# Two sliding-window attention layers on one core: values paired with the next group's scores up to group 57, a planner's transfer model switched later, requests for product inputs moved

## The chip, the core and the metric

The kernel runs on one core of a Trainium2 chip. The metric is the device time of one execution in microseconds. Three runs before the change took 1801.02, 1803.50 and 1804.85 us; the median is 1803.5.

The core has five engines with instruction streams of their own: TensorE (PE for its matmuls, PEld for its weight loads), VectorE (DVE), ScalarE (ACT), GpSimd (POOL) and SyncE (SP). The last three also issue DMAs here. A stream is executed in order; semaphores tie the streams together.

## The reference

Two attention layers over 2048 rows of width 1024, with 32 heads of 32, all in float32. Both project the input, attend inside a window, and project again.

```python
def _A_ref(x, wqkv, wo):                 # H = 32, Dh = 32, W = 8, dil = 2
    qkv = (x @ wqkv).reshape(B, S, 3, H, Dh).transpose(2, 0, 3, 1, 4)
    q, k, v = qkv[0], qkv[1], qkv[2]
    idx = pos[:, None] - (jnp.arange(W) * dil)[None, :]        # 8 keys, every second row back
    kg, vg = k[:, :, idx_c, :], v[:, :, idx_c, :]
    logits = einsum("bhsd,bhswd->bhsw", q, kg) * Dh ** -0.5    # rows before 0 masked
    o = einsum("bhsw,bhswd->bhsd", softmax(logits), vg)
    return o.transpose(0, 2, 1, 3).reshape(B, S, D) @ wo

def _B_ref(x, wqkv, wo):                 # the same with a causal window of 256 rows
    scores = einsum("bhqd,bhkd->bhqk", q, k) * Dh ** -0.5
    mask = (i - j >= 0) & (i - j < 256)
    o = einsum("bhqk,bhkd->bhqd", softmax(where(mask, scores, -1e9)), v)
    return o.transpose(0, 2, 1, 3).reshape(B, S, D) @ wo

return jnp.concatenate([A, B], axis=-1)
```

## The kernel before

**Arithmetic.** A float32 operand of a projection is kept as two parts for TensorE, a high one (a rounding cast, line 276 on ACT or line 279 on DVE) and a low one (`raw` minus high, line 282, always DVE, 512 columns an instruction). Each projection step is three matmuls (`TERMS`: high x high, high x low, low x high). Here a **step** is such an item of the list `gemm`; where a place in the program is given as a number, it counts these steps from the start.

**Tiling.** Layer B runs first, then layer A. Each layer is cut into four units of 512 rows, so there are units 0 to 3 (B, dense window) and 4 to 7 (A; its rows are put in an order in which the dilated window is a band of eight neighbours). A unit has eight groups of four heads; group hg = 8u + s. Groups 32 to 63 belong to layer A. `DU` = 4 is the number of layer B's units.

**The list of projections.** `plan` sets the order of the steps: for each group a Q/K block `qk(u, s)` of two halves t = 0, 1 with eight steps each; `v` for values; for the unit pair 6 and 7 the values come from seven block products instead (`vp`, `value_product`, tiles `r` holding sums of inputs, adds at line 1007); `o` is the output projection of layer B; `p` are the output products of layer A (adds at line 902); `x` steps bring in a unit's inputs. Line 1101 and line 1133 build sums for these products. A last run of projections closes the kernel behind the values of group 63.

**The loads.** A `Stream` walks through the projections' operands in their order of use. `load_to` issues a 512 KB load into one of three buffers `raw` on POOL's queue (line 221); `split_to(n)` makes the two parts of all operands up to the n-th (`parts`), and when the low part is done the buffer is free and the load three further on is issued. Operands have kinds: `w` a weight tile, `x` an input tile, `xw` the sums for a product. `qk_items` holds the calls of `split_to` by which a Q/K block requests the operands behind it; `then` is the index of the first operand behind the block's own, and k the step of the half.

**A group in layer A** (`window`). Scores are 64 small matmuls into four banks (`s<-pbuf`). DVE and ACT then do a chain: four mask adds (line 1214), row maximum `nm` (1224), subtraction (1226), exp on ACT (1230), row sum `sm` (1238), reciprocal (1240), product (1242), a transpose (1244), and ACT's eight copies into `wide` (1253, 1256). Values (`o<-wide,vbuf`) are 20 matmuls, or 16 in a unit without rows ahead of it. Q and K reach the scores by a copy from PSUM to `nat` and a DMA on SP's queue into `pbuf` (`pbuf<-nat`, the seat). In layer B the keys go to `kst` by such DMAs.

**What sets the order.** The order of all engines is fixed when the program is built. A planner keeps a clock for each engine (class `Clock`, with a table of costs) and at each point takes the next step of the projections, the next scores or the next values, whichever is ready first. Its `ready` functions hold the rules. `PAIRED` appears in three of them: scores of a group below `PAIRED` wait until the group before has its weights in `wide`; values of a group are not issued before the scores of the next one, as long as that one is below `PAIRED`; and a scores item below `PAIRED` has its reserve of instructions raised by that of the values behind it.

```python
if hg + 1 < PAIRED and hg + 1 not in done["scores"]:
    return None
```

So up to group 49 the values of a group come directly behind the scores of the next; from 50 on each comes when it is ready.

**The transfers in the planner.** `marks` are two places in the list of steps. Between them `ck.traced` is set; then the planner takes a load's time from a model in which two queues share the transfer engines (`share`), outside from one in which transfers follow each other (`move`). The flag also picks the rule for POOL's use of the port that it has in common with DVE. It is a matter of what the planner expects; the program issues the same instructions either way.

Of the kernel before, what the change touches and what calls it, by code (L numbers as in the profile page):

```python
# [29 lines left out]
CHUNK, ASKED, LEFT, FETCHED = 256, 150, 290, 7.0  # L30
EXTRA, EACH = 246, 5.2
P_LATE = 1.5
PAIRED = 50
VPARTS = ((0,4),(4,2),(6,2))
V_SLOTS = {0:0,5:1,7:2}
O_SLOTS = {2: (0, 1), 3: (2, 3), 4: (4, 5), 5: (6, 7)}
# [255 lines left out]
def kernel(ctx, tc, xs, wqk, wv, wo, outs, units):  # L292
# [4 lines left out]
    DU = sum(u[2] for u in units)  # L297
# [21 lines left out]
    def mm(out, left, right, **k):  # L319
        issued[0] += 4 if left.dtype == F32 else 2  # L320
        n = int(issued[0] + EXTRA - ASKED) // CHUNK
        if n > asked[0]:
            asked[:] = n, ck.now
        nc.tensor.matmul(out, left, right, **k)  # L324
# [90 lines left out]
    for p in plan:  # L415
# [21 lines left out]
        else:  # L437
# [8 lines left out]
            else:  # L446
# [6 lines left out]
    st = Stream(nc, ck, raws, wpool, xpool, items, [more[:, 1024 * i:1024 * i + 1024] for i in range(3)],  # L453
                where[("qk",) + LIGHT_FROM + (0,)] if LIGHT_FROM[0] < U else len(items))
# [109 lines left out]
    def latest(*ts):  # L564
        return None if any(t is None for t in ts) else max(ts)


    def qk_items(u, s):
# [98 lines left out]
        for t in range(2):  # L667
            h = {}

            def ready(k, t=t, h=h):  # L670
                if k == 0:
                    st.split_to(where["qk", u, s, t] + 1)
                    w = st.ready[where["qk", u, s, t]]
                    h["r"] = w if isinstance(w, list) else [w, w]
                    return latest(rg.when(), h["r"][0], xready[u][0])
                if k >= len(xready[u]):
                    return None
                if k == NK - 1 and nat + t >= NN and (dense or t == 0):
                    n = done["nat"].get(nat + t - NN)
                    return n and max(xready[u][k], n - 0.6)  # L680
                return max(xready[u][k], h["r"][k // 4])

            def run(k, t=t, h=h):
                if k == 0:
                    h["ps"], h["b"] = rg.take()
                    h["w"], _ = st.get(where["qk", u, s, t])
                for i, (a, b) in enumerate(TERMS):
                    mm(h["ps"], h["w"][:, a, k * P:(k + 1) * P], xt[u][k][:, b, :],
                                     start=(k == 0 and i == 0), stop=(k == NK - 1 and i == 2))
                then = where["qk", u, s, t] + 1  # L690
                if t == 1 and s == 0 and u:
                    then = max(then, st.split)
                kinds = [kind for kind, _ in st.items[then:then + 2]]
                if k == ASK and kinds and kinds[0] not in ("x", "xw"):
                    st.split_to(then + 1)
                if k == ASK and t == 0 and u > DU and kinds[:1] == ["x"] and st.split >= where["qk", u, s, 1]:
                    st.split_to(where["qk", u, s, 1] + 1)
                if kinds[:1] == ["xw"] and k in (0, 2, 4, 6):
                    st.split_to(then + 1 + k // 2)
                if kinds == ["w", "w"] and k == 5 and (then in firsts or then + 1 in firsts):  # L700
                    st.split_to(then + 2)
                if kinds == ["w", "xw"] and k == 6:
                    st.split_to(then + 2)
                if k in (4, 6) and kinds[:1] == ["xt"]:
                    st.split_to(then + k // 2)
                if k == 6 and t == 1 and not hg:
                    st.split_to(7)

            def after(k, t=t, h=h):
                if k == NK - 1:  # L710
                    evac(t, h["ps"], h["b"])

            for k in range(NK):
                out.append((lambda k=k, ready=ready: ready(k), lambda k=k, run=run: run(k), 3 * CG,
                            lambda k=k, after=after: after(k)))
# [446 lines left out]
    def x_items(u):  # L1162
        xt[u], xready[u] = [], []

        def run(g):
            a, b = st.get(where["x", u, g])
            xt[u] += a
            xready[u] += b

        return [[(lambda: 0.0, lambda g=g: run(g), 0.0, lambda: None)] for g in range(4)]  # L1170


    def window(u, s):
# [18 lines left out]
        def scores_ready():  # L1192
            if last_dense + 1 < hg < PAIRED and hg - 1 not in done["p"]:
                return None
            return latest(rs.empty(), done["stack"].get((u, s)), done["p"][hg - 1] + P_LATE if last_dense + 1 < hg < PAIRED else 0.0,
                          done["clear"].get(buf) if hg - 2 <= last_dense else done["o"].get(hg - 2))
# [62 lines left out]
        def values_ready():  # L1259
            if hg + 1 < PAIRED and hg + 1 not in done["scores"]:  # L1260
                return None
            return latest(done["v"].get((u, vp)), h.get("p") and h["p"] + P_LATE, ro.when())
# [14 lines left out]

        return [Item(scores_ready, scores, CW, 256 + (16 * len(kbs) if hg < PAIRED else 0))], [Item(values_ready, values, C3 + 0.9, 16 * len(kbs))]

# [260 lines left out]
    def fill(at, n):  # L1540

        def run():
            mm(ps, idle[:, :P], idle, start=True, stop=True)

        def after(last):
            if last:
                rs.give(bank, ck.now + ck.SEM)

        return [(lambda: 0.0, run, CG, lambda i=i: after(at == FILL[-1][0] and i == n - 1)) for i in range(n)]
# [8 lines left out]
    x1 = None  # L1558
    marks = []
    for p in plan:  # L1560
        if not marks and p[1] >= DU:
            marks.append(len(gemm))
        if len(marks) == 1 and p[0] == "p":
            marks.append(len(gemm))
        if p[0] == "qk":
            new = qk_items(p[1], p[2])
            if p == ("qk", 0, 0):
                q, k, x = new[:NK], new[NK:], x_items(0)
                f = dict(FILL)
                new = x[0] + sum([q[i:i + 1] + fill(i + 1, f.get(i + 1, 0)) for i in range(4)], [])  # L1570
                for i in (1, 2, 3):
                    new[new.index(q[2 * i]) if i < 2 else len(new):0] = x[i]
                    if i == 1:
                        new += k[:4]
                    else:
                        new += q[2 * i:2 * i + 2] + k[2 * i:2 * i + 2]
            if p[1:] == (0, NG - 1):
                x1 = x1 or x_items(1)
                for g in range(3, FIRST_X - 1, -1):
                    new[NK + 2 * g - 2:NK + 2 * g - 2] = x1[g]  # L1580
            gemm += new
        elif p[0] == "v":
            new = v_items(p[1], p[2])
            if p[1:] == (0, 2) and FIRST_X:
                x1 = x_items(1)
                for g in range(FIRST_X - 1, -1, -1):
                    new[X1_AT[g]:X1_AT[g]] = x1[g]
            elif V_SLOTS.get(NG - 1) == p[2] and 0 < p[1] < U - 1:
                m = 2 * VPARTS[p[2]][1]
                for g, x in reversed(list(enumerate(x_items(p[1] + 1)))):  # L1590
                    new[m * g + XAT:m * g + XAT] = x
            gemm += new
        elif p[0] == "o":
            gemm += o_items(p[1], p[2])
        elif p[0] == "p":
            gemm += product(p[1], p[2])
        elif p[0] == "vp":
            new = value_product(p[2])
            if VP_AT.get((p[1], NG - 1)) == p[2:] and p[1] + 1 < U:
                for g, x in reversed(list(enumerate(x_items(p[1] + 1)))):  # L1600
                    new[4 * g + XAT:4 * g + XAT] = x
            gemm += new
# [87 lines left out]
```

## Time and profile before

| | |
|---|---|
| median of three runs | 1803.5 us (1801.02 to 1804.85) |
| the profiled execution's own time | 1798.77 us |
| its span, first to last instruction | 1796.8 us |
| mean granted clock of TensorE | 0.998 |
| TensorE matmuls | 14496 records, 1774.0 us, 99% |
| VectorE | 1297.5 us, 72% |
| ScalarE | 943.7 us, 53% |
| GpSimd | 411.8 us, 23% |
| DMA | 324.57 MB, mean 181 GB/s |

The span lies 2 us inside the execution's own time. A row of the timeline has the start, the time to the end of the last instruction in the row, the engine, line and operation, output and inputs, and in brackets the idle time ahead of it with what ended it. The chain that ended last has start, duration, engine, output, line and the count of instructions. All matmuls are recorded at line 324, so they are told apart by their tiles: `g` projections, `s` scores, `o` values.

### The profile page before, as it was taken

The numbers are of one execution on the slowest core, as the hardware profiler recorded it, in microseconds if no ns is written. First come the engines' busy times: TensorE is split into PE (matmuls) and PEld (weight loads), VectorE is DVE, ScalarE is ACT, GpSimd is POOL, SyncE is SP. The second block draws the span as 40 slices with busy tenths as digits, with TensorE's granted clock in tenths as the row PEclk, the third lists the DMA queues.
The fourth block names the chain that finished last, engine by engine and source line by source line (L and its number), as shares of the span: only waits on it lengthen the run. The fifth ranks groups of instructions, "written<-read, shape, count | busy, mean of one in ns | idle before, by whom it ended". The sixth has DMA issues, their size and how long they took to land.

```text
span 1796.8 us, 38440 instructions
## 1 busy us (share of the span) xinstructions
PE 1774.0 (99%) x14496; PEld 1442.6 (80%) x14496; DVE 1297.5 (72%) x2877; ACT 943.7 (53%) x2337; POOL 411.8 (23%) x961
## 2 busy tenths in 40 slices
PE   9999999999999999999999999999999999999999
PEld 7787778888778888878787788888888787887887
DVE  6777876768867769867678556766666768868866
ACT  5565566555656555656554524543464435355442
POOL 3322323222332222332223400101010101001120
PEclk9999999999999999999999999999999999999999
DMA  8354664645645556555556166766576667848984
GB/s 257 106 147 136 185 167 136 166 136 145 185 141 161 152 134 169 152 146 149 145 134 185 48 202 197 226 204 186 183 226 192 198 196 254 291 139 280 346 280 144
DMA packets 154793, 324.57 MB, mean 181 GB/s; under 512 B 18032, under 2 KB 58992, under 8 KB 154608
## 3 DMA queue, kind: packets, MB, share of 16 engines
q0 software_dynamic: 45792, 166.74, 30.5%
q1 hardware_dynamic: 98736, 137.02, 26.8%
q10 hardware_dynamic: 10080, 18.35, 2.8%
q8 instruction: 115, 1.88, 0.4%
q14 instruction: 70, 0.57, 0.1%
HBM read 201.33 MB, written 53.48 MB: 142 GB/s over the span
## 4 chain that ended last, share of the span: by engine, by line
PE 88%; DVE 4%; DMA 3%; issue 3%; ACT 1%; SPq 0%; POOL 0%; DVEq 0%; ACTq 0%; POOLq 0%
PE g L324 69%; PE s L324 13%; PE o L324 6%; DVE w L282 1%; DMA raw<-xs 1%; DMA raw<-tv 1%; DMA kst<-nat 1%; ACT s L1393 0%; DMA pbuf<-nat 0%; DVE x L282 0%; ACT w L276 0%; DVE r L1101 0%; DVE band L1242 0%; DMA qst<-nat 0%; DVE w L279 0%
## 5 line engine op out<-in xcount | busy, mean ns | idle before, releaser
L324 PE MATMUL g<-x,w 128*128 128x512 f32 x3552 | 876.2, 393 | 2.2 <-DVE w L282 0.7
L324 PEld LDWEIGHTS g<-x,w 128*128 128x128 f32 x3552 | 656.5, 188 | 131.6 <-issue 5.8
L282 DVE TENSOR_TENSOR w<-raw,w 128x512 fp32r<-128x512 f32 x510 | 334.1, 697 | 53.8 <-ACT w L276 47.3
L1393 ACT ACTIVATE s<-s,nm 128x384 f32<-128x384 f32 (+2 forms) x512 | 274.3, 537 | 118.4 <-DVE nm L1388 112.0
L1388 DVE CUSTOM_DVE_ANT_0 s<-s,mask_d 128x384 f32<-128x384 f32 (+2 forms) x512 | 261.9, 554 | 90.5 <-PE s L324 90.2
L324 PE MATMUL g<-w,x 128*128 128x256 f32 (+1 forms) x1728 | 308.9, 327 | 3.3 <-DVE w L279 1.8
L1452 POOL TENSOR_SCALAR_AFFINE_SELECT pbuf<-pbuf 128x128 f32<-128x128 f32 (+1 forms) x604 | 218.8, 390 | 315.1 <-ACT pbuf L1473 313.5
L324 PEld LDWEIGHTS g<-w,x 128*128 128x128 f32 x1728 | 256.3, 191 | 29.2 <-DVE w L282 2.7
L324 PE MATMUL g<-r,w 128*128 128x512 f32 x960 | 238.2, 393 | 0.5 <-DVE r L1352 0.5
L1473 ACT ACTIVATE pbuf<-s 128x384 f32<-128x384 f32 (+2 forms) x480 | 203.7, 504 | 62.6 <-PE s L324 60.3
L324 PEld LDWEIGHTS g<-r,w 128*128 128x128 f32 x960 | 177.3, 188 | 35.9 <-DVE r L1352 1.1
L221 POOL DMA_DIRECT2D raw<-wqk x126 | 68.1, 540 | 359.4 <-DVE w L282 241.9
L324 PEld LDWEIGHTS s<-qst,kst 128*128 128x128 f32 x704 | 113.9, 189 | 42.5 <-ACT s L1393 17.4
L324 PE MATMUL s<-kst,qst 96*128 96x384 f32 (+2 forms) x512 | 143.0, 343 | 3.5 <-DMA kst<-nat 2.6
L324 PE MATMUL s<-qst,kst 128*128 128x256 f32 (+2 forms) x704 | 137.2, 302 | 4.0 <-ACT s L1393 3.2
L276 ACT CAST w<-raw 128x1024 fp32r<-128x1024 f32 (+1 forms) x89 | 92.0, 1038 | 67.0 <-PE g L324 29.9
L279 DVE CAST w<-raw 128x1024 fp32r<-128x1024 f32 x167 | 115.7, 693 | 15.7 <-PE g L324 10.5
L324 PEld LDWEIGHTS s<-kst,qst 96*128 96x128 f32 x512 | 93.9, 189 | 29.1 <-issue 7.6
L1393 ACT ACTIVATION_READ_ACCUMULATOR s<-s,nm 128x1 f32 x512 | 105.3, 206 | 0.0
L1253 ACT COPY wide<-band 32x512 f32<-32x512 f32 x128 | 79.0, 617 | 25.0 <-DVE band L1244 23.6
L324 PE MATMUL o<-pbuf,vbuf 128*32 128x384 f32 (+2 forms) x1408 | 91.1, 388 | 0.0
L282 DVE TENSOR_TENSOR x<-raw,x 128x512 fp32r<-128x512 f32 x116 | 75.6, 689 | 21.2 <-ACT x L276 19.9
(91 smaller groups left out, 1394.1 us busy)
## 6 DMA issues: line engine op xcount, KB each, us to landing
raw<-wqk POOLq DMA_DIRECT2D x126, 512.0 KB, 4.8
raw<-wv POOLq DMA_DIRECT2D x60, 512.0 KB, 5.1
qst<-nat SPq DMA_DIRECT2D x96, 256.0 KB, 3.1
kst<-nat SPq DMA_DIRECT2D x96, 256.0 KB, 4.8
raw<-wo POOLq DMA_DIRECT2D x44, 512.0 KB, 4.5
raw<-xs POOLq DMA_DIRECT2D x28, 512.0 KB, 4.6
outs<-ost ACTq DMA_DIRECT2D x38, 256.0 KB, 2.5
kst<-halo SPq DMA_DIRECT2D x72, 128.0 KB, 4.7
```

The source lines that it names most:

```text
L221: (self.nc.scalar if early else self.nc.gpsimd).dma_start(raw if len(ap.shape) == 2 else raw.rearrange("p (a b) -> p a b", a=2), ap)
L276: nc.scalar.copy(t[:, 0, :], raw)
L279: nc.vector.tensor_copy(t[:, 0, :], raw)
L282: nc.vector.tensor_tensor(t[:, 1, c:c + 512], raw[:, c:c + 512], t[:, 0, c:c + 512].bitcast(F32), op=ALU.subtract)
L324: nc.tensor.matmul(out, left, right, **k)
L1253: nc.scalar.copy(diag[r:r + 32, :, :, c:c + 32], turned[r:r + 32, :, :, 1, :])
L1388: nc.vector.tensor_tensor_reduce(ps[:, :n], ps[:, :n], mask[:, cut:full], scale=-1.0, scalar=BIG, op0=ALU.add, op1=ALU.min, accum_out=nm)
L1393: nc.scalar.activation(ps[:, :n], ps[:, :n], AF.Exp, bias=nm, scale=-1.0, accum_out=sm)
L1452: nc.gpsimd.affine_select(w, w, pattern=[[0, m], [step, n]], compare_op=ALU.is_ge, fill=0.0, base=base, channel_multiplier=chan)
L1473: nc.scalar.activation(w, ps[:, :pack * n].rearrange("p (j n) -> p j n", j=pack), AF.Exp)
```

## The change

Three edits. `PAIRED` goes from 50 to 57, so that the values of groups 49 to 55 also wait for the scores of the next group, and the scores of 50 to 56 for the group before. In `qk_items` the requests for product sums (`xw`) are made in three portions at steps 0, 2 and 4 of a half, each reaching one operand further, in place of four at 0, 2, 4 and 6; and the request for a weight followed by a sum is made at step 3 in place of 6. The first mark of the shared model of transfers goes from the first entry of layer A in the plan to the Q/K block of group (4, 2).

```diff
-PAIRED = 50
+PAIRED = 57
...
-                if kinds[:1] == ["xw"] and k in (0, 2, 4, 6):
-                    st.split_to(then + 1 + k // 2)
+                if kinds[:1] == ["xw"] and k in (0, 2, 4):
+                    st.split_to(then + 2 + k // 2)
                 if kinds == ["w", "w"] and k == 5 and (then in firsts or then + 1 in firsts):
                     st.split_to(then + 2)
-                if kinds == ["w", "xw"] and k == 6:
+                if kinds == ["w", "xw"] and k == 3:
                     st.split_to(then + 2)
...
     for p in plan:
-        if not marks and p[1] >= DU:
+        if not marks and p[1:] == (DU, 2) and p[0] == "qk":
             marks.append(len(gemm))
```

The instructions are the same in number and kind, apart from which of ACT and DVE does some of the casts. Their order is the same until the end of layer B; the changes lie in layer A. Three places show them.

PE at the end of unit 6, from the projections behind the scores of group 49 (`vbuf` the values, `wide` the attention weights). Before:

```order
L324 MATMUL g<-w,r 128x512 x12
L324 MATMUL o<-wide,vbuf_127 32x136 x12
L324 MATMUL o<-wide,vbuf_127 32x128 x4
L324 MATMUL g<-w,r 128x512 x30
L324 MATMUL s<-pbuf 32x40 x64
L324 MATMUL g<-w,r 128x512 x6
L324 MATMUL g<-x,w 128x512 x48
L324 MATMUL g<-w,r 128x512 x6
L324 MATMUL o<-wide,vbuf_127 32x136 x12
L324 MATMUL o<-wide,vbuf_127 32x128 x4
```

After, PE's rows from the same place on:

```order
L324 MATMUL g<-w,r 128x512 x48
L324 MATMUL g<-x,w 128x512 x9
L324 MATMUL s<-pbuf 32x40 x64
L324 MATMUL o<-wide,vbuf_127 32x136 x12
L324 MATMUL o<-wide,vbuf_127 32x128 x4
L324 MATMUL g<-x,w 128x512 x39
L324 MATMUL g<-w,r 128x512 x36
L324 MATMUL s<-pbuf 32x40 x64
L324 MATMUL o<-wide,vbuf_127 32x136 x12
L324 MATMUL o<-wide,vbuf_127 32x128 x4
```

Before, the values of 49 and the scores of 50 stand 30 matmuls apart, and the values of 50 stand alone. Now the scores of 50 and the values of 49 stand together, 15 matmuls later than the scores did, and 75 further on the scores of 51 and the values of 50.

DVE at value product 6, from the mask adds of group 50. Before:

```order
L1214 TENSOR_TENSOR band<-s,near 128x4x40 x4
L1007 TENSOR_TENSOR r<-g,r 128x512
L1224 TENSOR_REDUCE nm<-band 128x16
L1226 TENSOR_TENSOR band<-band,nm 128x16x40
L1238 TENSOR_REDUCE sm<-band 128x16
L1240 RECIPROCAL sm<-sm 128x16
L1242 TENSOR_TENSOR band<-band,sm 128x16x40
L1244 STREAM_TRANSPOSE band<-band 128x1024
L282 TENSOR_TENSOR r<-raw,r 128x512 x2
L279 CAST w<-raw 128x1024
L282 TENSOR_TENSOR w<-raw,w 128x512 x2
L1101 TENSOR_TENSOR r<-r 128x256 x4
```

After, DVE's rows from the same mask adds on:

```order
L1214 TENSOR_TENSOR band<-s,near 128x4x40 x4
L282 TENSOR_TENSOR r<-raw,r 128x512 x2
L1224 TENSOR_REDUCE nm<-band 128x16
L1226 TENSOR_TENSOR band<-band,nm 128x16x40
L282 TENSOR_TENSOR w<-raw,w 128x512 x2
L282 TENSOR_TENSOR r<-raw,r 128x512 x2
L1238 TENSOR_REDUCE sm<-band 128x16
L1240 RECIPROCAL sm<-sm 128x16
L1242 TENSOR_TENSOR band<-band,sm 128x16x40
L1244 STREAM_TRANSPOSE band<-band 128x1024
L282 TENSOR_TENSOR w<-raw,w 128x512 x2
L1101 TENSOR_TENSOR r<-r 128x256 x4
```

The splits that stood behind the chain of group 50 (`r` and `w` from `raw`) now stand between its parts: one directly behind the mask adds, two behind the subtraction, one behind the transpose. The cast of a weight has left DVE for ACT, and the product add (1007) that stood behind the mask adds now stands ahead of them.

DVE between value products 3 and 4, behind the splits of the sums. Before, starting with the mask adds of group 54:

```order
L1214 TENSOR_TENSOR band<-s,near 128x4x40 x4
L282 TENSOR_TENSOR w<-raw,w 128x512 x2
L1224 TENSOR_REDUCE nm<-band 128x16
L1226 TENSOR_TENSOR band<-band,nm 128x16x40
L282 TENSOR_TENSOR w<-raw,w 128x512 x2
L282 TENSOR_TENSOR x<-raw,x 128x512 x2
L1007 TENSOR_TENSOR r<-g,r 128x512 x2
L282 TENSOR_TENSOR x<-raw,x 128x512 x2
L1238 TENSOR_REDUCE sm<-band 128x16
L1240 RECIPROCAL sm<-sm 128x16
L1242 TENSOR_TENSOR band<-band,sm 128x16x40
L1244 STREAM_TRANSPOSE band<-band 128x1024
```

After, at the same splits:

```order
L282 TENSOR_TENSOR w<-raw,w 128x512 x2
L279 CAST w<-raw 128x1024
L282 TENSOR_TENSOR w<-raw,w 128x512 x2
L282 TENSOR_TENSOR x<-raw,x 128x512 x2
L1007 TENSOR_TENSOR r<-g,r 128x512 x2
L282 TENSOR_TENSOR x<-raw,x 128x512 x2
L1007 TENSOR_TENSOR r<-g,r 128x512 x2
L282 TENSOR_TENSOR x<-raw,x 128x512 x2
L1007 TENSOR_TENSOR r<-g,r 128x512 x2
L282 TENSOR_TENSOR x<-raw,x 128x512 x2
L1007 TENSOR_TENSOR r<-g,r 128x512 x2
L1214 TENSOR_TENSOR band<-s,near 128x4x40 x4
```

The chain of group 54 that stood among the splits of unit 7's inputs (`x`) and the adds of product 3 has moved behind them.

The planner's places for scores and values, in steps from the program's start:

| group | scores before | after | values before | after |
|---|---|---|---|---|
| 49 | 1520 | 1520 | 1542 | 1557 |
| 50 | 1552 | 1557 | 1572 | 1582 |
| 53 | 1632 | 1638 | 1650 | 1672 |
| 54 | 1647 | 1672 | 1676 | 1703 |
| 55 | 1668 | 1703 | 1694 | 1734 |
| 56 | 1697 | 1734 | 1719 | 1752 |
| 57 | 1730 | 1741 | 1751 | 1762 |
| 58 | 1751 | 1761 | 1771 | 1777 |
| 59 | 1760 | 1768 | 1783 | 1786 |
| 60 | 1781 | 1777 | 1799 | 1797 |
| 61 | 1794 | 1795 | 1813 | 1814 |
| 62 | 1810 | 1812 | 1829 | 1837 |
| 63 | 1828 | 1826 | 1855 | 1855 |

## The prediction

> **What bounds the kernel now.** I read the busy shares of the page first, then busy time by stretch (the windows), then the chain that ended last, and last the timeline of PE with what ended each of its waits.
>
> ```profile
> span 1796.8 us, 38440 instructions
> ...
> PE 1774.0 (99%) x14496; PEld 1442.6 (80%) x14496; DVE 1297.5 (72%) x2877; ACT 943.7 (53%) x2337; POOL 411.8 (23%) x961
> ```
>
> ```profile
> 1190.00:1310.00 120.00, 120.00 (x1506) 100.29 (x1505) 74.46 (x134) 49.21 (x93) 11.47 (x26) 1.00 0.63 191
> 1440.00:1480.00 40.00, 40.00 (x503) 32.42 (x504) 25.15 (x47) 15.98 (x31) 3.70 (x7) 1.00 0.58 187
> 1480.00:1530.00 50.00, 47.34 (x617) 37.36 (x603) 42.13 (x71) 29.07 (x57) 6.88 (x13) 1.00 0.77 247
> 1530.00:1600.00 70.00, 70.00 (x924) 56.63 (x923) 50.43 (x84) 30.45 (x57) 5.29 (x10) 1.00 0.70 235
> 982.40:986.00 3.60, 3.55 (x10) 3.03 (x10) 3.57 (x7) 0.00 (x0) 0.55 (x1) 0.53 0.87 261
> ```
>
> The window columns are: stretch, its length, then busy time and records of PE, PEld, DVE, ACT and POOL, the granted clock, the DMA share, GB/s. TensorE is the bound. In the 120 us from 1190 on it never stops, and it stops only where DVE is nearly full: from 1480 to 1530 DVE is busy for 42.13 of 50 us (0.84) and PE loses 2.66 us. At 0.63 and 0.72 (1440 to 1480, 1530 to 1600) it loses nothing. A change of order that leaves the instructions alone can therefore bring only two things: fewer changes between kinds of matmul, and fewer waits of PE.
>
> **The price of a visit.** Two kinds of row in the chain that ended last give it.
>
> ```profile
> 1390.52 1.25 PE s L324 x109
> 1391.77 1.05 PE o L324 x32
> ...
> 1409.83 7.02 PE g L324 x30
> 1416.86 1.25 PE s L324 x104
> 1418.11 13.82 PE g L324 x60
> 1431.93 1.09 PE o L324 x32
> ...
> 1667.94 124.72 PE g L324 x549
> ```
>
> The last 549 projection matmuls go at 124.72 / 549 = 0.2272 us each. Thirty of them between a values visit and a scores visit take 7.02 us, which is 0.20 over 30 x 0.2272, and sixty take 13.82, which is 0.19 over. So a run of projections that stands between two visits costs 0.20 us beyond its matmuls. Scores cost 1.25 us with values right behind them (1390.52) and alone (1416.86), and values 1.05 and 1.09. A pair of visits thus saves one such 0.20. The change pairs scores of groups 50 to 56 with the values of the group before: seven pairs, **-1.4 us**.
>
> The Trainium skill (TensorEngine Tiling (Array Packing), Key Properties) says that changing the tiling mode drains TensorE. Scores to values is such a change too, so by it a pair saves one drain of four and keeps one inside; at half of the 0.20 for each drain this would be -0.7 in place of -1.4. The rows disagree: values behind scores cost no more than behind projections (1.05 against 1.09), and I keep -1.4.
>
> **The waits, one by one.** The rows are PE's timeline in layer A, with the idle time ahead of a row in brackets.
>
> ```profile
> 982.45 1.22 PE L324 MATMUL s<-kst,qst 96*128 96x384 f32 x3 [2.60 <-DMA kst<-nat]
> ...
> 1341.89 4.15 PE L324 MATMUL g<-w,x 128*128 128x512 f32 x17 [1.32 <-DVE w L282]
> ...
> 1379.78 1.52 PE L324 MATMUL g<-w,r 128*128 128x512 f32 x6
> 1381.54 0.50 PE L324 MATMUL g<-w,r 128*128 128x512 f32 x1 [0.25 <-ACT w L276]
> 1382.27 8.25 PE L324 MATMUL g<-w,r 128*128 128x512 f32 x35 [0.23 <-DVE w L282]
> ...
> 1433.03 0.50 PE L324 MATMUL g<-w,r 128*128 128x512 f32 x1
> 1434.36 8.23 PE L324 MATMUL g<-w,r 128*128 128x512 f32 x35 [0.83 <-DVE w L282]
> ...
> 1510.29 4.33 PE L324 MATMUL g<-x,w 128*128 128x512 f32 x18 [0.65 <-DVE r L1007]
> ...
> 1522.53 1.52 PE L324 MATMUL g<-w,x 128*128 128x512 f32 x6
> 1525.83 0.49 PE L324 MATMUL g<-w,x 128*128 128x512 f32 x1 [1.78 <-DVE w L279]
> 1526.55 4.17 PE L324 MATMUL g<-w,x 128*128 128x512 f32 x17 [0.23 <-DVE w L282]
> ...
> 1643.56 0.23 PE L324 MATMUL s<-pbuf 32*32 32x40 f32 x2 [0.65 <-DMA od<-r]
> 1644.02 0.70 PE L324 MATMUL s<-pbuf 32*32 32x40 f32 x56 [0.23 <-DMA pbuf<-nat]
> ...
> 1660.02 5.29 PE L324 MATMUL g<-x,w 128*128 128x512 f32 x22 [0.49 <-DVE w L282]
> 1665.89 0.93 PE L324 MATMUL g<-x,w 128*128 128x512 f32 x3 [0.59 <-DVE band L902]
> ```
>
> A wait costs a little more than its brackets. From 1522.53 to 1526.55 seven matmuls need 7 x 0.2272 = 1.59, and 4.02 us pass: 2.43, with 2.01 in brackets. Likewise 1379.78 to 1382.27 loses 0.90, and 1433.03 to 1434.36 loses 1.33 - 0.23 = 1.10.
>
> Which of them go depends on DVE, where one softmax chain of a group occupies:
>
> ```profile
> L1244 DVE STREAM_TRANSPOSE band<-band 128x1024 f32<-128x1024 f32 x18 | 22.4, 1245 | 0.6
> L1214 DVE TENSOR_TENSOR band<-s,near 128x160 f32<-128x160 f32 x68 | 17.2, 316 | 27.7 <-PE s L324 27.7
> ...
> L1242 DVE TENSOR_TENSOR band<-band,sm 128x640 f32<-128x640 f32 x17 | 14.0, 825 | 0.6
> L1226 DVE TENSOR_TENSOR band<-band,nm 128x640 f32<-128x640 f32 x17 | 14.0, 825 | 0.6
> L1238 DVE TENSOR_REDUCE sm<-band 128x16 f32<-128x640 f32 x17 | 13.9, 815 | 6.8 <-ACT band L1230 6.8
> L1224 DVE TENSOR_REDUCE nm<-band 128x16 f32<-128x640 f32 x17 | 13.8, 814 | 0.2
> ...
> L1240 DVE RECIPROCAL sm<-sm 128x16 f32<-128x16 f32 x17 | 4.3, 253 | 0.6
> ```
>
> This is 1.25 + 17.2/17 + 2 x 0.83 + 2 x 0.81 + 0.25 = 5.8 us.
>
> *Value product 6 (1434.36, 1.10).* Its last weight is late by a chain of reuse:
>
> ```profile
> 1426.35 1.25 DVE L282 TENSOR_TENSOR r<-raw,r 128x512 fp32r<-128x512 f32 x2
> ...
> 1433.01 1.29 DVE L282 TENSOR_TENSOR w<-raw,w 128x512 fp32r<-128x512 f32 x2 [0.56 <-PE o L324]
> ```
> ```profile
> 1427.90 0.72 POOL L221 DMA_DIRECT2D raw<-wv  x1 [7.55 <-DVE r L282]
> ```
>
> The load is issued only when DVE has split an earlier tile and so freed its buffer, and DVE does that split behind the whole chain of group 50. In the changed order the split of that tile stands right behind the four mask adds, some 6 us earlier, and the weight's own low part right behind the transpose. **-1.1.**
>
> *Value product 4 (1526.55, 2.43) and product 3's banks (1510.29, 0.65).* Both lie in the full stretch of DVE. There the changed order has the scores of group 54 later by 25 steps (a step is three projection matmuls, so 17 us), those of 55 by 35 and those of 56 by 37. One chain of 5.8 us leaves the 50 us: 36.3 / 50 = 0.73, the level at which nothing is lost. **-3.1.**
>
> *Products 0 and 2 (1341.89, 1.32; 1381.54, 0.90).* For the first, the masks of group 46 come ahead of the low part of an x tile and fill a gap in DVE; I count half, **-0.7**. For the second, the weight is requested ahead of the scores of 47 in place of behind them, **-0.9**.
>
> *The last waits.* The scores of 63 come two steps earlier and the values of 62 eight steps later: the weight at 1660.02 (0.49) then has its split ahead of that chain, **-0.5**. The scores of 63 wait for a seat whose DMA follows the last Q/K block, which stays where it is, so 0.88 stays; the 0.59 at 1665.89 stays too.
>
> *The clock's marks and 982.45.* The changed model of transfers begins later in unit 4. The scores that wait there keep their place in the order, 24 steps behind the block that feeds them, and I leave the wait as it is: 0. It is dearer than 2.60, since the window from 982.40 has a granted clock of 0.53. The Trainium skill (TensorE: Matmul & The Clock Gate, Part 1) puts the slow clock behind an idle window of some 3.4 us; by that no wait here would cost more than its length. The trace disagrees, at 2.60 us; it is the one such place in the rows above.
>
> *Moved requests on the queues.* The same loads are issued on POOL's queue, one or two steps earlier; POOL is busy for 5.29 of 70 us there, and SP's seats do not move past them in the program. I take 0, between -0.3 (one step less of waiting, twice 0.23 saved) and +0.65 (a transfer like the one at 1643.56 made late).
>
> Gone: 1.4 + 1.1 + 3.1 + 0.7 + 0.9 + 0.5 = 7.7.
>
> **What comes new.** The groups that were put off are caught up later: scores of 57 to 60 now stand at steps 1741, 1761, 1768 and 1777, before at 1730, 1751, 1760 and 1781. From 1741 to 1777 is 36 x 3 x 0.2272 = 24.5 us and six visits, about 31 us. From 1530 to 1600 DVE has four chains (23.2) and other work of 27.2, so 0.39 per us. Three chains and that work make 17.4 + 12.1 = 29.5 of 31 us, a load of 0.95. At the loss of the 0.84 stretch (2.66 in 50) this gives 1.7; at twice that, 3.3. I take 2.5, between 0 (the planner's fillers fit, as at 0.72) and 9 (below).
>
> The sum is -7.7 + 2.5 = -5.2. The profiled execution took 1798.77 us, so it would take 1793.6; the median of the runs shown is 1803.5, 4.7 above that execution, and goes to **1798.3**.
>
> **The rivals.** *The waits only move.* DVE does the same work; what leaves 1480 to 1530 is lost again in unit 7 (3.3 for 2.5), product 6 and product 2 still wait because the raw buffer and not the request sets the load (2.0 not gained), and that part of the change does nothing. For it: 1427.90 is issued by a freed buffer. Against: the split itself moves. Result -5.2 + 0.8 + 2.0 = -2.4, 1801.1.
>
> *Slower.* From the scores of 57 on DVE falls behind, and every later weight and every values visit waits for it. Scores 58 to values 58 is 16 steps (10.9 us) and three visits (3.6), 14.5 us, and group 50's last copy for its values ended 12.1 us behind its scores (1418.11):
>
> ```profile
> 1429.91 0.29 ACT L1256 COPY wide<-band 32x128 f32<-32x128 f32 x1
> ```
>
> The margin is 2.4 us, and the next chain starts within it. If each of 57 to 60 stalls by the largest price of this stage, 2.43, it costs 9.7, and a backlog that lasts to group 61 costs 2.43 once more: 12.1 - 7.7 = +4.4, 1807.9. It decides from 11.3 us of new waits on. Against it: waits drain a backlog, and the excess of DVE over 31 us is near 0, not 12.
>
> *The wait at 982.45 goes too.* The transfers ahead of it are issued otherwise, and 2.60 + 6 x 0.2 (half clock) = 3.8 more is saved: 1794.5.
>
> **How the numbers follow.** 0.2% (3.6 us) is about what a measurement of this kernel can tell from no change. The forecast (1795 to 1799.9) has 0.49, the 982 case 0.10, waits that only move 0.24, slower 0.17. Faster by over 0.2% is 0.59, within 0.24, slower 0.17. The range for 8 in 10 goes from 1794.0 (the 982 case) to 1807.0 (new waits of 11 us); the forecast's own is 1794.5 to 1801.
>
> **What would show it.** In the changed profile: PE without a wait from 1505 to 1530 and DVE near 0.73 there; no wait in product 6 (near 1434); S and o rows adjacent up to group 56; DVE over 0.9 in the 31 us ahead of 1600 and new waits of one to three us there. A sum of waits between 1340 and 1668 that is not below that of before by 4 us, or new waits over 8 us, would make it wrong.

## The result, and the profile after

The changed kernel takes 1797.17 us (median of 13 runs, 1793.53 to 1801.12) against 1803.51 us for the kernel before: a ratio of 0.9964, 95% interval 0.9956 to 0.9973. Its profiled execution took 1798.31 us, only 0.46 less than the profiled execution before (1798.77). So the two profiles alone do not show the 6.3 us; the experiments below show which of the three edits carries them, and only in part where.

The page of the changed kernel, the counterpart of the first fence of the prediction:

```profile
span 1796.6 us, 38462 instructions
...
PE 1772.1 (99%) x14496; PEld 1441.6 (80%) x14496; DVE 1298.1 (72%) x2877; ACT 940.0 (52%) x2335; POOL 413.9 (23%) x963
```

PE is busy 1.9 us less for the same 14496 records; part of that is the granted clock (last section). The windows of the same stretches, in the same columns, and one more for the part in which the late groups are caught up:

```profile
1480.00:1530.00 50.00, 48.40 (x506) 38.60 (x506) 40.27 (x68) 24.52 (x49) 7.41 (x14) 1.00 0.81 269
1530.00:1600.00 70.00, 70.00 (x1195) 56.63 (x1196) 52.26 (x88) 33.58 (x62) 5.28 (x10) 1.00 0.69 225
1566.00:1595.00 29.00, 29.00 (x562) 23.30 (x562) 21.45 (x37) 17.97 (x36) 2.12 (x4) 1.00 0.55 168
```

From 1480 to 1530 PE now loses 1.60 us in place of 2.66, with DVE at 0.81. In the stretch that the prediction feared, 1566 to 1595, PE loses nothing and DVE stands at 0.74, not 0.95. Over the whole part in which the prediction summed its waits, before and then after:

```profile
1340.00:1668.00 328.00, 320.47 (x4014) 255.88 (x4013) 243.31 (x419) 164.84 (x309) 39.24 (x72) 1.00 0.69 224
1340.00:1668.00 328.00, 320.21 (x4024) 257.63 (x4023) 248.18 (x427) 161.77 (x306) 39.44 (x72) 1.00 0.69 225
```

PE is idle for 7.53 us of it before and for 7.79 after: in this pair of profiles the waits have moved and have not become fewer.

PE's timeline of the changed kernel, the rows behind waits:

```profile
980.15 0.76 PE L324 MATMUL s<-kst,qst 96*128 96x384 f32 x3 [0.42 <-issue]
...
1165.12 4.81 PE L324 MATMUL g<-w,x 128*128 128x512 f32 x20 [2.90 <-DVE w L282]
...
1343.57 1.65 PE L324 MATMUL g<-w,x 128*128 128x512 f32 x6 [1.01 <-DVE w L282]
1345.50 2.11 PE L324 MATMUL g<-w,x 128*128 128x512 f32 x8 [0.28 <-DVE w L282]
...
1366.61 0.30 PE L324 MATMUL s<-pbuf 32*32 32x40 f32 x15 [0.87 <-issue]
...
1385.21 2.13 PE L324 MATMUL g<-w,r 128*128 128x512 f32 x8 [0.22 <-DVE w L282]
...
1435.62 6.87 PE L324 MATMUL g<-w,r 128*128 128x512 f32 x29 [1.46 <-DVE w L282]
...
1505.05 3.04 PE L324 MATMUL g<-w,r 128*128 128x512 f32 x12 [0.39 <-DVE r L1007]
...
1524.22 0.49 PE L324 MATMUL g<-w,x 128*128 128x512 f32 x1 [0.75 <-DVE w L279]
1524.95 5.28 PE L324 MATMUL g<-w,x 128*128 128x512 f32 x22 [0.23 <-DVE w L282]
...
1642.04 0.23 PE L324 MATMUL s<-pbuf 32*32 32x40 f32 x2 [0.85 <-DMA pbuf<-nat]
1642.66 1.26 PE L324 MATMUL s<-pbuf 32*32 32x40 f32 x122 [0.39 <-DMA pbuf<-nat]
...
1665.68 0.92 PE L324 MATMUL g<-x,w 128*128 128x512 f32 x3 [1.10 <-DVE band L902]
```

Two things stand out. The wait at 982 has shrunk from 2.60 to 0.42, and one of 2.90 that the kernel before did not have stands at 1165. And at value product 6 the wait is not gone but longer (1435.62: 1.46; before 0.83).

### The profile page after: what moved, and what is told of

Read it like the earlier page. It is cut to its first block, busy times and chain, and to the rows that moved or that the text cites. A ratio compares the mean times of both kernels' runs of the same rounds, so it can differ in the third digit from the quotient of the medians.

```text
span 1796.6 us, 38462 instructions
## 1 busy us (share of the span) xinstructions
PE 1772.1 (99%) x14496; PEld 1441.6 (80%) x14496; DVE 1298.1 (72%) x2877; ACT 940.0 (52%) x2335; POOL 413.9 (23%) x963
## 4 chain that ended last, share of the span: by engine, by line
PE 89%; DMA 4%; DVE 3%; issue 2%; ACT 2%; POOL 0%; SPq 0%; DVEq 0%; POOLq 0%; ACTq 0%
PE g L324 70%; PE s L324 13%; PE o L324 6%; DVE w L282 1%; DMA raw<-xs 1%; DMA raw<-wqk 1%; DMA raw<-tv 1%; ACT s L1393 0%; DMA outs<-ost 0%; DMA pbuf<-nat 0%; ACT w L276 0%; POOL pbuf L1452 0%; DMA qst<-nat 0%; DVE band L1242 0%; DVE sm L1238 0%
## 5 line engine op out<-in xcount | busy, mean ns | idle before, releaser
L279 DVE CAST w<-raw 128x1024 fp32r<-128x1024 f32 x174 | 120.3, 691 | 8.3 <-PE g L324 5.8
L276 ACT CAST w<-raw 128x1024 fp32r<-128x1024 f32 (+1 forms) x82 | 84.8, 1038 | 58.6 <-PE g L324 27.6
L1214 DVE TENSOR_TENSOR band<-s,near 128x160 f32<-128x160 f32 x128 | 32.5, 316 | 86.4 <-PE s L324 79.9
```

Of the source, the lines that this page charges most:

```text
L276: nc.scalar.copy(t[:, 0, :], raw)
L279: nc.vector.tensor_copy(t[:, 0, :], raw)
L1214: nc.vector.tensor_tensor(p64()[:, j, :, 24:], banks[j][0][:, :160].rearrange("p (b c) -> p b c", b=4), m, op=ALU.add)
```

## The experiments

**All combinations of the three edits.** The order listings of the parts show that they hardly touch one another's places: the mark changes PE's order only from the end of layer B to the scores of group 48, PAIRED and the requests only from there on. So the eight combinations form a table. Each kernel was timed against the kernel before on the same chip. The chips differ (the median of the kernel before lies between 1801.80 and 1803.58), so the ratios are what to compare, not the medians. The last two columns are times between the starts of two projection matmuls, counted from zero, in each one's single profile: from the 3200th to the 4300th (units 4 and early 5, with the waits that the mark changes), and from the 5030th to the 6026th (units 6 and 7, where the other two act).

| kernel | median, us | ratio to before (95%) | 3200 to 4300 | 5030 to 6026 |
|---|---|---|---|---|
| before | 1803.51 | 1 | 273.62 | 276.98 |
| e1: PAIRED | 1797.98 | 0.9972 (0.9956 to 0.9987) | 272.45 | 278.31 |
| e2: requests | 1798.25 | 0.9964 (0.9950 to 0.9978) | 274.72 | 273.31 |
| e3: mark | 1801.49 | 0.9991 (0.9977 to 1.0005) | 275.54 | 274.44 |
| e4: PAIRED, requests | 1798.63 | 0.9972 (0.9956 to 0.9988) | 276.55 | 273.88 |
| e5: PAIRED, mark | 1800.00 | 0.9982 (0.9972 to 0.9993) | 275.63 | 274.53 |
| e6: requests, mark | 1796.00 | 0.9964 (0.9950 to 0.9978) | 276.33 | 272.69 |
| the whole change | 1797.17 | 0.9964 (0.9956 to 0.9973) | 276.00 | 273.81 |

*e1_paired.*

```diff
-PAIRED = 50
+PAIRED = 57
```

> PAIRED = 57 alone, the other two edits left out. By the prediction this part brings 1.4 (seven visits) + 3.1 (products 3 and 4) + 0.5 (the weight at 1660) + part of the 1.1 at product 6, less 2.5 of new waits: 2.5 to 3.6 us faster than before (ratio 0.998 to 0.9986). Rival, the mark carries the gain: within 1.5 us of before. Rival, visits alone count and the waits only move: 1.4 us faster, and waits between 1340 and 1668 sum to the 8 us of before.

It was 0.9972, more than the 0.998 to 0.9986 of the prediction's split, though its interval covers them all; and its profile does not show the gain where that split put it: 5030 to 6026 took 1.3 us longer than before, with 2.18 and 0.82 of waiting at product 6.

*e2_requests.*

```diff
-                if kinds[:1] == ["xw"] and k in (0, 2, 4, 6):
-                    st.split_to(then + 1 + k // 2)
+                if kinds[:1] == ["xw"] and k in (0, 2, 4):
+                    st.split_to(then + 2 + k // 2)
...
-                if kinds == ["w", "xw"] and k == 6:
+                if kinds == ["w", "xw"] and k == 3:
```

> The moved requests alone. By the prediction 0.9 (product 2) + 0.7 (product 0) + some of product 6: 1.6 to 2.7 us faster (ratio 0.9985 to 0.9991). Rival, the raw buffer and not the request sets the load: 0, and the waits at products 2 and 6 stay at 0.5 and 0.8 in brackets.

0.9964: more than expected, and as much as the whole change. The rival of the raw buffer falls at product 6, which has no wait in this profile. At product 2 it does not: 0.80 stands there in brackets, more than the 0.48 of before.

*e3_mark.*

```diff
-        if not marks and p[1] >= DU:
+        if not marks and p[1:] == (DU, 2) and p[0] == "qk":
```

> The first mark alone; it changes the order only between the scores of group 33 and those of 48. By the prediction 0 within 1 us. Rival, the mark carries the gain: 3 us or more faster (ratio under 0.9983), with the wait at 982 or one near 1165 changed in the profile.

0.9991 (0.9977 to 1.0005), not told from 1: the mark does not carry the gain.

*e4_paired_requests* (the edits of e1 and e2).

> PAIRED and the requests without the mark; from the scores of group 49 on the order is that of the whole change. By the prediction all of its 5 to 6 us (ratio 0.9965 to 0.9973). Rival, the mark carries half or more: 3 us or less (0.9983 or above).

0.9972 lies at the prediction's edge (0.9973) and excludes the rival's 0.9983 by the middle value only; the interval reaches 0.9988.

*e5_paired_mark* (e1 and e3) and *e6_req_mark* (e2 and e3).

> PAIRED = 57 and the mark, without the requests; with the four runs before it fills the table of all combinations. If PAIRED and the requests each take away the same waits and the mark is worth nothing, it is 4 to 6 us faster than before (0.9967 to 0.9978). By the prediction's split (PAIRED about 3, requests about 2, mark 0) it is 3 us faster (0.9983).

> The requests and the mark, PAIRED left at 50. If the parts overlap: 5 to 6.5 us faster (0.9964 to 0.9972). By the prediction's split 2 us faster (0.9989). In both cases the profile should show the wait of some 2.9 us near 1165 that stood in the two profiles with the mark, and none of over 1 us near 982.

e5 came out at 0.9982, where the prediction's split had it. e6 at 0.9964 is what the requests give alone. Over the four pairs of the table that differ in one edit, the requests are worth 0.0036, 0.0000, 0.0027 and 0.0018, in the mean 0.0020 or 3.6 us; PAIRED 0.0028, 0.0009, -0.0008 and 0.0000, in the mean 0.0007 or 1.3 us, and nothing where the requests are in; the mark 0.0009, -0.0010, 0.0000 and 0.0008, in the mean 0.0002. The intervals of single cells are some 0.0010 to 0.0015 wide to either side; taken as independent they leave each of these means some 0.0009 to either side (an estimate). So the gain of the requests is shown, and neither PAIRED nor the mark is told from nothing by its mean; the order of the three is not shown either. The stage times point the same way: 5030 to 6026 takes 273.4 in the mean of the four profiles with the requests and 276.1 in the four without, but single profiles of the four without lie between 274.4 and 278.3.

*e9_sums* and *e10_weight* split the requests into their two lines.

```diff
-                if kinds[:1] == ["xw"] and k in (0, 2, 4, 6):
-                    st.split_to(then + 1 + k // 2)
+                if kinds[:1] == ["xw"] and k in (0, 2, 4):
+                    st.split_to(then + 2 + k // 2)
```

> Of the requests only the sums' part (three portions at steps 0, 2 and 4, one operand further). If it is this part that frees the loads of products 2 and 6: 5 to 6 us faster than before (0.9967 to 0.9972). If the weight's request at step 3 does it: within 1.5 us of before.

```diff
-                if kinds == ["w", "xw"] and k == 6:
+                if kinds == ["w", "xw"] and k == 3:
```

> Of the requests only the other part (a weight followed by a sum requested at step 3 in place of 6). If it carries the gain: 5 to 6 us faster than before; if the sums' part does: within 1.5 us.

Ratios of 0.9988 (0.9975 to 1.0001) and 0.9984 (0.9973 to 0.9995): neither line carries the gain alone, and both expectations of "this part and not that" fall. Together they would make 0.9972, which is inside e2's interval (0.9950 to 0.9978). In the profiles the weight's request alone leaves no wait at product 6, the sums' part alone leaves 0.49.

*e8_mark_41.* The wait at 982 was gone (in the changed kernel 0.42) in every profile with the mark, and the new one at 1165 was in every one of them (2.81 to 2.92). If these cancel, a mark one block earlier should have the first order without the second.

```diff
-        if not marks and p[1] >= DU:
+        if not marks and p[1:] == (DU, 1) and p[0] == "qk":
```

(with the requests of e2, PAIRED at 50)

> The requests, PAIRED left at 50, and the mark at the Q/K block of group (4, 1) in place of (4, 2). The order around 982 is then that of the runs with the mark, and that around 1165 that of before. If the mark's zero is a gain at 982 (2.6 to 4.0 us and a stretch of half clock) cancelled by the new wait of 2.9 at 1165, both are gone here: 2.5 to 4 us faster than requests and mark (e6), so 9 to 10 us faster than before (ratio 0.9945 to 0.995). Rival: the wait near 1165 has another cause and stays, 0.9964.

1791.85 us, 0.9942 (0.9926 to 0.9957): the cancelling is shown, and this kernel beats the whole change by 0.0022 in the ratios, 4.0 us (5.3 between medians of two chips). From the 3200th to the 4300th projection it takes 271.35 against 276.33 in e6 and 276.00 in the changed kernel; a wait of 1.53 at 1054 is left in that part. PE's timeline of e8 at the two places, now without brackets:

```profile
978.73 0.69 PE L324 MATMUL s<-kst,qst 96*128 96x384 f32 x3
...
1159.45 2.88 PE L324 MATMUL g<-w,x 128*128 128x512 f32 x12
```

*e12_41_paired* adds PAIRED = 57 to it.

> The whole change, PAIRED = 57 included, with the mark at the Q/K block of group (4, 1): it differs from e8 in PAIRED alone, and from the whole change in the mark alone. If PAIRED adds nothing to the requests (seven visits saved, as much lost in new waits): within 1.5 us of e8 (0.9934 to 0.995). By the prediction's terms for it (1.4 + 3.1 + 0.5 - 2.5) it is 2.5 us faster than e8 (0.9928). Rival: PAIRED costs, 2 us or more slower than e8 (0.9953 or above). Against the whole change it should be 4 to 6 us faster, by the waits at 982 and 1165.

1791.86 us, 0.9950 (0.9936 to 0.9964), against 0.9942 for e8, each on its own chip. The intervals overlap by far: on top of the requests no gain of PAIRED is seen, though it saves seven visits, nor is a cost of 2 us excluded. Against the whole change it is 0.0014 faster, 2.5 us, less than the 4 to 6 expected, though the intervals allow for that too.

*e7_all_paired* pushes PAIRED to the end, on the whole change.

```diff
-PAIRED = 57
+PAIRED = 64
```

> The whole change with PAIRED = 64, so that every group up to 63 is paired; scores of 57 to 63 then come 70 to 130 projection matmuls later, those of 63 at 6027 of 6576 in place of 5940. By the price of a visit (0.20 each, six more pairs) 1.2 us faster than the whole change, so 7 to 8 us faster than before (0.9955 to 0.9961). Rival: DVE has the last chains and the sums for the last products on top of each other, and the last run of projections waits for them: slower than the whole change by 2 us or more.

1827.39 us, 1.0139 (1.0120 to 1.0158): slower than before by 24 us, a miss of the expected gain; the rival had the sign, not the cause. PE's timeline, and a window across it:

```profile
1623.09 0.57 PE L324 MATMUL s<-pbuf 32*32 32x40 f32 x40 [1.63 <-issue]
1627.28 0.30 PE L324 MATMUL o<-wide,vbuf 128*32 128x8 f32 x8 [3.62 <-ACT wide L1256]
1630.16 2.01 PE L324 MATMUL o<-wide,vbuf 128*32 128x136 f32 x32 [2.58 <-ACT wide L1256]
1634.62 2.93 PE L324 MATMUL g<-x,w 128*128 128x512 f32 x6 [2.45 <-ACT w L276]
```
```profile
1620.00:1690.00 70.00, 45.33 (x637) 34.59 (x630) 39.06 (x65) 33.99 (x62) 9.33 (x16) 0.76 0.59 194
```

Two scores and the values behind them stand in a row with no projection between, so a whole chain lies bare, twice. DVE is busy for only 39.06 of these 70 us: it is not full, it is waited for. Between the 5030th and the 6026th projection e7 takes 303.48 us, 29.7 more than the changed kernel. PE's idle time there grows by 22.9 of these (from 5.40 to 28.30); the other 6.8 are longer busy time, with the clock at 0.76.

*e11_before_again.* The kernel before, for a second profile.

> The kernel before once more, for a second profile of the same order. If the waits of its first profile are its typical ones, the same ones stand there within 0.5 us each (982, products 0, 2, 4, 6) and the time is near 1799. If that profile was a lucky one, waits in products 2 to 6 are longer or stretches of half clock follow them, and the time is near 1803.

1800.10 us. The same places wait, and not by the same amount: 982 by 2.06 (2.60), product 0 by 2.16 (1.32), product 4 by 1.41 (1.78). And a stretch of half clock has come that the first profile lacked, behind product 4 (second row; the columns are those of the windows):

```profile
982.00:986.00 4.00, 4.00 (x13) 3.17 (x12) 3.95 (x10) 0.60 (x3) 0.55 (x1) 0.59 0.84 275
1528.00:1532.00 4.00, 4.00 (x12) 3.09 (x12) 3.37 (x5) 1.18 (x3) 0.16 (x1) 0.57 0.90 248
```

So the first profile was a favourable one; the second lies under the median of 1803.5 too. Over all 73 runs of the kernel before with a recorded clock, on four chips, the mean granted clock is 0.9973, over 13 of the changed one 0.9982; the difference is 0.0009 x 1797 = 1.6 us of the 6.3. The mean of the kernel before runs from 0.9968 to 0.9982 between these chips, so the clock's share of the gain may be anything from nothing to some 2.5 us. That fewer half-clock stretches behind shorter waits are part of the gain is therefore not shown; runs without a profile do not show where they lost time.

## Why the prediction was right, point by point

The sum was -5.2 us and the measurement -6.3, inside the range. The sign holds. That the size came out is in good part luck, for the prediction's own signs mostly failed. Scores and values do stand together up to group 56. But PE loses 1.26 us from 1505 to 1530, product 6 waits, DVE is busy for 21.26 of the 31 us ahead of 1600 (0.69, not over 0.9), and the waits from 1340 to 1668, which had to fall by 4 us, went from 7.53 to 7.79. The favourable first profile is a part of this: between the same two matmuls, the 4820th and the 6030th projection, PE is idle for 7.53 and 8.83 us in the two profiles of the kernel before and for 7.79 in that of the changed one. Against neither do the waits fall by the 4 us. In the profiles the change looks like the rival in which the waits only move, whose time of 1801.1 the runs exclude. The profiles show visits saved, waits moved and a half-clock price beside both; where the rest of the 6.3 us was saved in the runs without a profile stays open.

**The visits (-1.4): there, and spent again.** PE's timeline of the changed kernel shows the first new pair, scores of 50 and values of 49:

```profile
1421.12 1.32 PE L324 MATMUL s<-pbuf 32*32 32x40 f32 x128
1422.37 1.12 PE L324 MATMUL o<-wide,vbuf 128*32 128x136 f32 x32
1423.42 9.15 PE L324 MATMUL g<-x,w 128*128 128x512 f32 x39
```

From 1421.12 to 1423.42 it takes 2.30 us, the 1.25 and 1.05 of the pair before, so values behind scores carry no extra cost. As a net gain it is not seen: given the requests, no gain of PAIRED is measured (e8 against e12). Five pairs of profiles differ in PAIRED alone (before and e1, e2 and e4, e3 and e5, e6 and the whole change, e8 and e12). From the 4820th to the 6030th projection PE's time without its waits and without the clock lost in stretches of half clock is 0.9 to 2.3 us shorter with PAIRED at 57, in the mean 1.7; its waits are 1.2 to 3.6 us longer. The next point shows one place.

**Product 6 (-1.1): wrong.** The step that failed is "the split of that tile stands right behind the four mask adds, some 6 us earlier". It stands there in DVE's order, but it waits for a cast that is behind something else on ACT, and the chain behind it waits with it. Rows of the changed kernel, ACT first, then POOL, then DVE:

```profile
1423.56 0.59 ACT L1326 COPY r<-o 128x512 f32<-128x512 f32 x1 [4.67 <-PE o L324]
1424.04 1.14 ACT L276 CAST r<-raw 128x512 fp32r<-128x512 f32 x2
...
1431.55 1.05 ACT L276 CAST w<-raw 128x1024 fp32r<-128x1024 f32 x1 [1.19 <-DMA raw<-wv]
```
```profile
1426.28 0.72 POOL L221 DMA_DIRECT2D raw<-wv  x1 [4.99 <-DVE r L282]
```
```profile
1424.69 1.29 DVE L282 TENSOR_TENSOR r<-raw,r 128x512 fp32r<-128x512 f32 x2 [1.25 <-ACT r L276]
...
1428.73 1.29 DVE L282 TENSOR_TENSOR w<-raw,w 128x512 fp32r<-128x512 f32 x2 [1.16 <-ACT w L276]
...
1433.14 1.25 DVE L1244 STREAM_TRANSPOSE band<-band 128x1024 f32<-128x1024 f32 x1
1434.31 1.25 DVE L282 TENSOR_TENSOR w<-raw,w 128x512 fp32r<-128x512 f32 x2
```

ACT stands 4.67 us before the copy of the values of group 49 out of PSUM (line 1326), since the pair has put those values behind the scores of 50; the cast of the sums is queued behind that copy, the low part behind the cast, the load behind the low part. The load goes out at 1426.28 and lands at 1431.5, and the weight's low part then waits for the rest of the chain, in which DVE has stood still for 1.25 and 1.16 us. The kernels reach this place at different times, so times are best counted from the start of the 5096th projection (1407.70 before, 1409.91 after, 1408.63 in e6): the load goes out 20.2 us behind it before and 16.4 after, so 3.8 us earlier and not 6. In e6, with the requests and without the pair, it goes out at 15.6, and DVE is through with the transpose 2.5 us sooner (the splits behind it begin at 21.9 in place of 24.4). PE runs through. POOL's, DVE's and PE's rows of e6:

```profile
1424.25 0.72 POOL L221 DMA_DIRECT2D raw<-wv  x1 [2.96 <-DVE r L282]
```
```profile
1430.55 1.25 DVE L282 TENSOR_TENSOR r<-raw,r 128x512 fp32r<-128x512 f32 x2
1431.72 1.28 DVE L282 TENSOR_TENSOR w<-raw,w 128x512 fp32r<-128x512 f32 x2
```
```profile
1431.33 5.87 PE L324 MATMUL g<-w,r 128*128 128x512 f32 x24
```

The other profiles agree: with PAIRED at 57 the brackets at product 6 sum to 1.46, 3.00, 1.46, 2.02 and 1.47 (the whole change, e1, e4, e5, e12), with both requests and PAIRED at 50 to nothing (e2, e6, e8). The last wait, at 1665, is 1.10 to 1.42 in those five and 0.56 to 0.60 in the other eight (e7 left out). So PAIRED costs about what it saves, 1.5 + 0.6 against 1.4 and what it gains at product 4. That ACT's queue is the cause at product 6 is read from the rows; a copy moved away from ACT was not tried.

**Products 3 and 4 (-3.1): a third.** In brackets 0.65 and 2.01 became 0.61 and 0.98, so 1.1 went. DVE fell to 0.81 and not to 0.73: the chain that left was partly replaced by other work. The chain's removal is also not needed: in e6, with PAIRED at 50, 0.17 is left at product 4, though a wait of 0.86 stands ahead of a values visit at 1516.

**Products 0 and 2 (-0.7, -0.9): not as said.** 1.32 became 1.29, and 0.48 became 0.22. Product 0 lies ahead of the first place at which PAIRED or the requests change any engine's order; in the seven profiles with the order of before there (before, e11, e1, e2, e4, e9, e10) it waits between 1.06 and 2.19. At product 2 the requests alone leave 0.80 (e2), so they do not take that wait away. The 0.87 that came new for the scores of group 47 is not of the change: e2 and e10 have the order of before up to there, and wait 0.74 and 1.00. The 0.49 at 1660 went (-0.5), as said.

**New waits (+2.5): wrong in place.** Three chains within 31 us were costed with other work at 0.39 us per us, a mean over 1530 to 1600. That other work lies in the first half of the stretch; where the chains are caught up there is little of it (of DVE's 21.45 us from 1566 to 1595, 6.5 are splits and casts, 0.22 per us), and PE lost nothing. What came new stands elsewhere: 0.63 more at 1435, 0.51 more at 1665, and the 0.87 at 1366 that also comes without the change, so 1.1 to 2.0 us.

**The mark (0): right as a sum, wrong as a reason.** "I leave the wait as it is" was false. The mark takes most of the wait at 982 away and brings one of 2.9 at 1165, where the scores and values now stand 6 to 12 projection matmuls later. At 982 the transfers moved; SP's rows of before, then of after, and POOL's of before, then of after:

```profile
968.81 2.61 SPq L649 DMA_DIRECT2D kst<-nat  x3
```
```profile
968.02 2.48 SPq L649 DMA_DIRECT2D kst<-nat  x3
```
```profile
970.42 0.72 POOL L221 DMA_DIRECT2D raw<-wv  x1 [1.45 <-DVE w L282]
974.46 0.80 POOL L221 DMA_DIRECT2D raw<-wv  x1 [3.31 <-DMA raw<-wv]
```
```profile
971.51 0.72 POOL L221 DMA_DIRECT2D raw<-wv  x1 [3.99 <-DVE w L282]
975.85 0.72 POOL L221 DMA_DIRECT2D raw<-wv  x1 [3.62 <-DVE w L282]
```

The keys' seats go out 0.8 us earlier and the two loads behind them 1.1 and 1.4 us later. Which of the two shortens the wait was not tried apart. The rival of the 982 case, given 0.10, was half true; e8 is that case without the other wait.

**The requests (1.6 to 2.7 in the split of e2): too small.** They measure 3.6 in the mean, some 1.6 to either side, and are the one part whose gain is shown. Of the waits that the prediction gave them (products 0, 2 and 6) only product 6's goes with them. In e2 products 3 and 4 wait for 0.59 us in place of 2.66 and 2.41 in the two profiles of before; but e3, with the order of before there, waits 0.99, so that this is theirs is not shown.

## What to carry to other kernels

An edit that shortens the bound engine's stream is worth what it saves only if what it moves is not awaited by an in-order queue: list, for each instruction that comes later, what stands behind its consumers on their engines. A part that measures zero can be two effects that cancel; its profile shows both, and an experiment one notch aside may keep one. And where runs spread by more than the effect, one profile before and one after can agree to 0.5 us while the medians differ by 6: count waits over several profiles of the same order.

## What the runs showed of the hardware

The clock halves for about 3.4 us behind waits shorter than that, and not each time. The length is worked out from the rows: 6 us at 0.72 lack 0.28 x 6 = 1.7 us of clock, which is half of 3.4. In e5 a wait of 2.81 and one of 1.32 + 0.23 were each followed by such a stretch, in the changed kernel the 2.90 was not (windows of e5, then of the changed kernel):

```profile
1163.00:1168.00 5.00, 4.94 (x15) 3.93 (x16) 3.80 (x7) 3.55 (x9) 2.13 (x4) 0.66 0.49 130
1384.00:1390.00 6.00, 5.97 (x19) 4.77 (x20) 1.44 (x3) 1.08 (x2) 0.53 (x1) 0.72 0.94 297
```
```profile
1164.00:1168.00 4.00, 2.88 (x13) 2.40 (x14) 3.93 (x7) 3.89 (x9) 1.42 (x2) 1.00 0.51 135
```

One such stretch costs about 1.4 us: between the 300th and the 1200th projection matmul the changed kernel takes 270.46 with one at 170 us, and e3 takes 269.03 without. The Trainium skill (TensorE: Matmul & The Clock Gate, Part 1) has the slow clock after an idle window of some 3.4 us; here it follows 1.55 us of idle time, and only the length of the stretch agrees. A wait therefore has a second price that is drawn anew in each run: in the kernel before, product 4's 1.78 + 0.23 had no such stretch behind it, and the 1.41 + 0.23 of the same order in e11 had one. The spread between runs goes with it: of the 24 runs of the kernel before on the chip of e1, the 11 with a mean granted clock of 0.996 took 1805.2 us in the mean, the 7 with 0.998 took 1801.0.
